# Row maxima split into high and low before the turn, one handover for unit 0, and four weight loads moved on SyncE

## The chip, the cores and the metric

The kernel runs on one core of one Trainium2 chip. The metric is device time in microseconds. The kernel before takes 1729.69 us (median of three runs, 1728.79 to 1730.18).

The five engines are named as the profile names them: PE is TensorE, with PEld its weight loads; DVE is VectorE, ACT ScalarE, POOL GpSimd and SP SyncE. SP computes nothing here; it issues the DMAs, one after the other, and waits in its queue for the data of each.

## The reference

One transformer block whose two layer norms are modulated by a condition vector `c`. All of it is float32.

```python
mod = (silu(c) @ w_mod).reshape(1, 6, 1, 512)
sa, ca, ga, sb, cb, gb = (mod[:, i] for i in range(6))
h = layernorm(x) * (1 + ca) + sa
x = x + ga * attention(h)          # 32 heads of 16, one shared key and value head
h = layernorm(x) * (1 + cb) + sb
x = x + gb * ((sigmoid(h @ w_gate) * (h @ w_up)) @ w_down)
```

with S = 2048 rows of D = 512, F = 1792, and attention as

```python
q = (h @ wq).reshape(1, S, 32, 16).transpose(0, 2, 1, 3)
k, v = h @ wk, h @ wv              # S x 16 each
scores = einsum("bhqd,bkd->bhqk", q, k) * 16 ** -0.5
o = einsum("bhqk,bkd->bhqd", softmax(scores, axis=-1), v)
return o.transpose(0, 2, 1, 3).reshape(1, S, 512) @ wo
```

The softmax subtracts the row's maximum over the 2048 keys, so each of the 32 x 2048 rows of scores needs its maximum before the exponentials are taken.

## The kernel before

**Units.** The attention is cut into 32 units: four query blocks of 512 rows (`b` = 0 to 3), and in each eight units of four heads. Every score is computed twice. A tile `sa` has 128 queries on the partitions and 512 keys in the row; VectorE reduces it to one maximum per query (`mx`). A unit has 64 such tiles. A tile `st` has 128 keys on the partitions and 512 queries in the row; ScalarE takes its exponential to `P`, and TensorE multiplies `P` with the values into `c`. `sa` tiles run A0 = 80 tiles ahead of the `st` tiles, that is one unit and a quarter.

**How a maximum gets into the exponential.** The query operand `qp` of a unit holds, beside the queries' high and low fp16 parts, two rows for the maxima: high part and low part, each in fp16 and divided by SM = 16. The product `st` thereby comes out with the maximum already subtracted. The way of a maximum from `mx` (query on the partition) to these rows (query along the row) is here called the handover. `max_end` has VectorE reduce four partial maxima of each of 16 columns to `m16`, 128x16; `max_rows` has TensorE turn it (fp32, by the identity matrix) into a score bank `pm`, copies it out, makes the two parts, and has SP write them to `qp` with four DMAs. In the steady part ScalarE copies it out and GpSimd makes the parts; in the opening VectorE makes them from the bank. In the steady part the handover of a unit is called one step after the last of its `sa` tiles: `max_end` before the step's scores, `max_rows` in its middle.

**Queries.** The query projection `q` (four 128-column groups per block, 12 matmuls each, three to a piece in the opening) is split into high and low, written to DRAM (`qD`), and read back in `qp`'s layout by six DMAs for each pair of units. All of this is issued by SP.

**Order.** Instructions on TensorE, VectorE and ScalarE keep the order in which the program writes them (`Ordered`, `keep`), as do those issued through `pool1` on GpSimd. Those issued through `pool` and `sp` are placed by the scheduler of the language. The opening, up to 108 us, is one written string of tokens, `PLAN`: `lm` loads 1 MB of `w_mod`, `lw` a part of `wq`, `lx` a block of `x`; `q` is a third of a query group, `QA` and `QL` its high and low part; `a` is an `sa` product and `x` its maximum; `pm`, `me`, `pr`, `m` use a loaded part of `w_mod`; `mx` is a handover of unit 0. In the opening there are four `sa` banks, afterwards three, and two for `st`.

**Steps.** After the opening each step takes 128 keys: four `st` and four `sa` tiles alternate, with the value product of an earlier step and one or more pieces of other work between them. In block 0 these are the query projections of the other blocks, while GpSimd splits the weights of the second half into fp16 high and low parts and SP writes them to DRAM (`wst`, `gw`, `wD`). From unit 8 on they are the output projection and the second half of the previous block.

Of the kernel before, what the change touches and what calls it, by code (L numbers as in the profile page):

```python
# [78 lines left out]
def adaln_mqa_glu_kernel(  # L79
# [105 lines left out]
    make_identity(nc, ident)  # L185
    mhalf = cp.tile([P, 1], F32, name="mhalf")
# [17 lines left out]
    def load_mod(i):  # L204
        t_ = pro.tile([P, NDC, D], F32, tag="wm", name="wm", bufs=4)
        sp.dma_start(t_, w_mod[:, i * D:(i + 1) * D].rearrange("(k p) n -> p k n", p=P))
        wmods[i] = t_
# [323 lines left out]
    def a_max(i, n, sa):  # L531
        kc, qt = n // 16, n // 4 % 4
        j, pr = heads[n % 4]
        dve.tensor_reduce(mxs[i][:, 2 * j + pr, qt, kc:kc + 1], sa, axis=AX.X, op=ALU.max)
        if i > 0 and n == 63:
            pend.append((i, 0, 4))
# [13 lines left out]
    def max_rows(i, t0, t1, m16):  # L550
        qp, pr0 = get_q(i)
        nt = t1 - t0
        n = 4 * nt
        pm = sbank("sa")
        pe.transpose(pm[:n, :P], m16, ident)
        mh = wp.tile([n, 2, P], F16, tag="mh", name="mh", bufs=4)
        if not first:
            m32 = wp.tile([n, P], F32, tag="m32", name="m32", bufs=4)
# [3 lines left out]
        else:  # L562
            dve.tensor_scalar(mh[:, 0], pm[:n, :P], 1.0 / SM, None, op0=ALU.mult)
            dve.scalar_tensor_tensor(mh[:, 1], pm[:n, :P], 1.0 / SM, mh[:, 0],
                                     op0=ALU.mult, op1=ALU.subtract)
        for j in range(2):
            for h in range(2):
                r = 64 * j + 48 + h
                sp.dma_start(qp[r:r + 1, pr0:pr0 + 2, t0 * P:t1 * P], mh[2 * nt * j:2 * nt * (j + 1), h, :])
# [279 lines left out]
    groups = {}  # L849
# [10 lines left out]
    def q_end(b, o):  # L860
# [9 lines left out]
              "a": a_next, "x": lambda: a_max(*held.pop(0)), "mx": lambda t: max_end(0, t, t + 1)(),  # L870
              "lw": load_wq, "lx": load_x, "lm": load_mod, "bl": lambda: blanks.append(blank(pool1))}
# [204 lines left out]
```

## Time and profile before

| | |
|---|---|
| median of three runs | 1729.69 us |
| profiled execution | 1730.8 us, its span 1729.0 us |
| mean granted clock | 0.991 |
| TensorE busy | 1689.2 us, 98% |
| TensorE weight loads | 574.4 us, 33% |
| VectorE busy | 1431.1 us, 83% |
| ScalarE busy | 1232.7 us, 71% |
| GpSimd busy | 610.7 us, 35% |

A trace is one profiled execution. In a list of instructions a row begins with the start in us and the length in us, then the engine, the line, the operation, `out<-in`, the shapes and the count. What stands in square brackets is how long the engine had been idle before it and who ended the wait. The line L128 stands for every instruction that went through `Ordered`. A row of SPq is a stretch of time that SP's queue spent issuing DMAs of one kind. A row of the chain of waits is a start, a length, an engine and a tile: the work that the end of the run depended on, in order of time.

### The profile page before, as it was taken

To read this page: it belongs to the slowest core of one execution; us is meant where nothing else is said; L and a number is where in the kernel's file an instruction comes from. 1 tells how busy PE (TensorE), PEld (TensorE's weight loads), DVE (VectorE), ACT (ScalarE), POOL (GpSimd) and SP (SyncE) were. 2 spreads that over 40 slices of the span, in tenths; PEclk is the share of its full clock that TensorE was granted. 3 is DMA by queue.
4 is the path that set the end of the run, shared out by engine and by line. 5 is a ranking of instruction groups with operands and counts; after the bars stand their busy time and mean duration, and the time that the engine had idled before them with its cause. 6 is when DMAs were issued, how large, how long until landed. Compare 5 with 4: busy or idle time off the path is not lost.

```text
span 1729.0 us, 34862 instructions
## 1 busy us (share of the span) xinstructions
PE 1689.2 (98%) x13971; PEld 574.4 (33%) x13971; DVE 1431.1 (83%) x2371; ACT 1232.7 (71%) x2253; POOL 610.7 (35%) x720
## 2 busy tenths in 40 slices
PE   6989999999999999999999999999999999999998
PEld 3423333233223333333333333333333333323443
DVE  8889999899998888888898998898898888931311
ACT  4448888788878777777778777777778777774100
POOL 4341463543454231332154232233254141231533
PEclk9899999999999999999999999999999999999999
DMA  8021332320101010111011110011101010111211
GB/s 284 1 89 35 107 97 79 114 93 23 57 24 44 30 51 11 38 45 36 26 41 32 41 48 15 26 48 49 33 23 51 30 56 5 30 50 56 76 59 49
DMA packets 66282, 90.88 MB, mean 53 GB/s; under 512 B 14800, under 2 KB 41424, under 8 KB 66120
## 3 DMA queue, kind: packets, MB, share of 16 engines
q1 hardware_dynamic: 66120, 88.66, 16.2%
q8 instruction: 109, 1.79, 0.4%
q14 instruction: 53, 0.43, 0.1%
HBM read 67.68 MB, written 16.22 MB: 49 GB/s over the span
## 4 chain that ended last, share of the span: by engine, by line
PE 87%; DVE 4%; DMA 3%; POOL 2%; ACT 2%; issue 1%; SPq 1%; POOLq 0%; ACTq 0%; DVEq 0%
PE c L128 27%; PE st L128 21%; PE pgu L128 12%; PE sa L128 9%; PE pd L128 5%; PE pgu L152 4%; DVE mx L128 3%; PE pq L128 2%; PE pd L152 2%; PE po L128 2%; ACT P L128 1%; DMA wst<-in_B_w_up_dram 1%; PE pt L128 1%; DMA xall<-in_A_x_dram 1%; PE po L152 1%
## 5 line engine op out<-in xcount | busy, mean ns | idle before, releaser
L128 DVE TENSOR_REDUCE mx<-sa 128x1 f32<-128x512 f32 x2048 | 1289.6, 685 | 121.2 <-PE sa L128 114.3
L128 ACT ACTIVATE P<-st 128x512 f32<-128x512 f32 x2048 | 1135.0, 596 | 285.7 <-PE sa L128 250.4
L128 PE MATMUL st<-qp,kp 64*128 64x512 f16 x2048 | 748.4, 380 | 9.5 <-DMA qp<-mh 5.3
L128 PE MATMUL sa<-kp,qp 64*128 64x512 f16 x2048 | 749.2, 384 | 7.4 <-DVE mx L128 4.0
L128 PE MATMUL c<-P,V 128*32 128x512 f32 (+1 forms) x5296 | 578.3, 509 | 0.9 <-ACT cs L128 0.2
L128 PEld LDWEIGHTS <-kp 64*128 64x128 f16 x2048 | 177.0, 94 | 510.4 <-issue 416.9
L128 PEld LDWEIGHTS <-qp 64*128 64x128 f16 x2048 | 186.5, 93 | 171.1 <-issue 79.9
L128 PE MATMUL pgu<-h2h,gw 64*128 64x512 f16 x1344 | 242.9, 376 | 0.0
L128 PEld LDWEIGHTS c<-P,V 128*32 128x32 f32 x5296 | 104.5, 108 | 189.1 <-issue 180.2
L796 POOL TENSOR_SCALAR th<-th 128x512 f32<-128x512 f32 x42 | 25.9, 617 | 353.7 <-ACT th L128 353.7
L128 PE MATMUL pgu<-h2l,gw 64*128 64x512 f16 x672 | 133.3, 376 | 0.0
L128 PEld LDWEIGHTS <-gw 64*128 64x128 f16 x2016 | 100.0, 94 | 81.6 <-issue 4.1
L152 PE MATMUL pgu<-h2h,gw 128*128 128x512 f16 x224 | 66.9, 379 | 1.2 <-POOL h2h L303 1.2
L497 POOL MEMSET qp<- 32x2048 f16 x28 | 50.3, 1798 | 49.5 <-issue 30.0
L802 POOL TENSOR_TENSOR gl<-th,gh 128x512 f16<-128x512 f32 x56 | 64.7, 1155 | 4.1
L790 ACT ACTIVATE th<-pgu 128x512 f32<-128x512 f32 x14 | 8.4, 597 | 79.3 <-PE pgu L152 79.3
L799 DVE SCALAR_TENSOR_TENSOR th<-th,pgu 128x512 f32<-128x512 f32 x14 | 9.6, 688 | 66.0 <-PE pgu L152 51.9
L272 POOL TENSOR_SCALAR wst<-wst 128x512 f32<-128x512 f32 x46 | 28.4, 618 | 98.9 <-DMA wst<-in_B_w_gate_dram 41.7
L128 DVE COPY u<-pgu 128x512 f32<-128x512 f32 x42 | 28.6, 681 | 38.6 <-PE st L128 22.6
L819 POOL TENSOR_TENSOR ot<-ot,gb 128x512 f32<-128x512 f32 x10 | 12.7, 1271 | 132.0 <-ACT ot L128 132.0
L659 POOL TENSOR_TENSOR raw<-raw,rb 128x512 f32<-128x512 f32 x15 | 19.1, 1272 | 105.4 <-DMA rb<-lD 67.4
L797 POOL TENSOR_TENSOR th<-th,u 128x512 f32<-128x512 f32 x42 | 53.3, 1270 | 3.5
(157 smaller groups left out, 1314.0 us busy)
## 6 DMA issues: line engine op xcount, KB each, us to landing
gw<-wD SPq DMA_DIRECT2D x56, 512.0 KB
wD<-gw SPq DMA_DIRECT2D x14, 512.0 KB
wm<-in_w_mod_dram SPq DMA_DIRECT2D x6, 1024.0 KB
qp<-qD SPq DMA_DIRECT2D x96, 64.0 KB
qD<-q SPq DMA_DIRECT2D x16, 256.0 KB
raw<-cs SPq DMA_DIRECT2D x128, 32.0 KB
xr<-in_A_x_dram SPq DMA_DIRECT2D x16, 256.0 KB
out_dram<-ot SPq DMA_DIRECT2D x16, 256.0 KB
```

The source lines that it names most:

```text
L128: return (lambda *a, **k: keep(f_(*a, **k))) if pinned else f_
L152: pe.matmul(self.bank, l_, r_, start=(n == 0), stop=(n == self.n - 1))
L272: pool.tensor_scalar(w_, w_, SW, 0.0, op0=ALU.mult, op1=ALU.add)
L497: eng.memset(qp[j:j + 32], 0.0)
L659: keep(pool.tensor_tensor(raw, raw, rb, op=ALU.mult))
L790: act.activation(th, p_, AF.Tanh, scale=0.5 / (SH * SW))
L796: pool.tensor_scalar(th, th, 1.0, 1.0, op0=ALU.add, op1=ALU.mult)
L797: pool.tensor_tensor(th, th, u_, op=ALU.mult)
L799: dve.scalar_tensor_tensor(th, th, 1.0, p_, op0=ALU.add, op1=ALU.mult)
L802: pool.tensor_tensor(lo, th, hi, op=ALU.subtract)
L819: pool.tensor_tensor(ot, ot, mods[5], op=ALU.mult)
```

## The change

Three things change together.

*The split.* `max_end` now lets VectorE make the two parts from the unturned `m16`, in a tile `mhl` of 128x2x16 fp16: one `tensor_scalar` for the high part, one `scalar_tensor_tensor` for the low part. `max_rows` turns both with one fp16 matmul against a new fp16 identity, `ident16`, into 32x128 of a score bank; ScalarE copies these to `mh` (fp16), and four DMAs write the rows as before. The two GpSimd instructions of a handover go, and so do VectorE's two in the opening. `ident16` is one more GpSimd instruction at the start.

*Unit 0.* Its four handovers of 128 queries each (`mx0` to `mx3`) become one for all 512, in two tokens: `mx` is VectorE's part, `my` TensorE's, ScalarE's and SP's. The last part of `PLAN` is written anew.

*The loads.* The four loads `lm4 lm3 lm2 lm5` move from the head of the plan to behind the first `a`, and are issued through `sp1`, which keeps the order of the program.

```diff
 PLAN = (
-    'lw0 lx2 lx3 lw1 lw2 lw3 lm4 lm3 lm2 lm5 pm1 S00 S01 me1 ...
+    'lw0 lx2 lx3 lw1 lw2 lw3 pm1 S00 S01 me1 ...
...
-    '... ra3 E12 a H13 rb3 pk10 x E13 pk11 '
+    '... ra3 E12 a lm4 lm3 lm2 lm5 H13 rb3 pk10 x E13 pk11 '
...
-    'x a q013 x a x a QA01 q020 mx0 a x q021 QL01 a x q022 x a q023 x a mx1 q030 QA02 x a q031 x a QL02 x a q032 x '
-    'a q033 mx2 x a q100 QA03 x a q101 x QL03 a x a q102 mx3 a x q103 x a QA10 q110 x a q111 x QL10 a x a q112 x a '
-    'q113 x a x a QA11 x a x a QL11 x a x a x a x x x '
+    'x a q013 x a x a QA01 q020 x a q021 x QL01 a x q022 x a a q023 x a q030 QA02 x a x a q031 x QL02 a q032 x a '
+    'q033 a x QA03 a q100 x a q101 mx QL03 x a my q102 x a x a q103 x a q110 QA10 x a q111 x a QL10 x a q112 x a '
+    'q113 x a x a QA11 x a x a QL11 x a x x x '
 )
...
+    ident16 = cp.tile([P, P], F16, name="ident16")
+    pool.tensor_scalar(ident16, ident, 1.0, 0.0, op0=ALU.mult, op1=ALU.add)
...
-            pend.append((i, 0, 4))
+            pend.append((i,))
...
-    def max_end(i, t0, t1):
-        nt = t1 - t0
-        n = 4 * nt
-        m16 = wp.tile([P, n], F32, tag="m16", name="m16", bufs=4)
-        dve.tensor_reduce(m16.rearrange("p (h t) -> p h t", t=nt), mxs[i][:, :, t0:t1, :], axis=AX.X, op=ALU.max)
-        return lambda: max_rows(i, t0, t1, m16)
+    def max_end(i):
+        m16 = wp.tile([P, 16], F32, tag="m16", name="m16", bufs=4)
+        mhl = wp.tile([P, 2, 16], F16, tag="mhl", name="mhl", bufs=4)
+        dve.tensor_reduce(m16.rearrange("p (h t) -> p h t", t=4), mxs[i], axis=AX.X, op=ALU.max)
+        dve.tensor_scalar(mhl[:, 0], m16, 1.0 / SM, None, op0=ALU.mult)
+        dve.scalar_tensor_tensor(mhl[:, 1], m16, 1.0 / SM, mhl[:, 0], op0=ALU.mult, op1=ALU.subtract)
+        return lambda: max_rows(i, mhl)
...
-        pe.transpose(pm[:n, :P], m16, ident)
...
-            act.activation(m32, pm[:n, :P], AF.Identity, scale=1.0 / SM)
-            pool.tensor_scalar(mh[:, 0], m32, 1.0, 0.0, op0=ALU.mult, op1=ALU.add)
-            pool.tensor_tensor(mh[:, 1], m32, mh[:, 0], op=ALU.subtract)
...
+        pe.matmul(pm[:32, :P], mhl.rearrange("p h m -> p (h m)"), ident16, start=True, stop=True)
+        mh = wp.tile([32, P], F16, tag="mh", name="mh", bufs=4)
+        act.activation(mh, pm[:32, :P], AF.Identity)
         for j in range(2):
             for h in range(2):
                 r = 64 * j + 48 + h
-                sp.dma_start(qp[r:r + 1, pr0:pr0 + 2, t0 * P:t1 * P], mh[2 * nt * j:2 * nt * (j + 1), h, :])
+                sp.dma_start(qp[r:r + 1, pr0:pr0 + 2, :], mh[16 * h + 8 * j:16 * h + 8 * j + 8, :])
```

The order of instructions shows three places. A row is the line, the operation, `out<-in`, the shape and, behind an x, how many stand in a row.

The first is SP's queue in the opening; `wm` is a loaded part of `w_mod`, `q_...` a split query group, `qp<-mh` the rows of maxima. Before:

```order
L206 DMA wm<-in_w_mod_dram 128x4x512 x4
L479 DMA qD<-q_308 128x2x512
L505 DMA qp<-qD 16x4x512 x6
L569 DMA qp<-mh 1x2x128 x4
L479 DMA qD<-q_990 128x2x512
L569 DMA qp<-mh 1x2x128 x4
L479 DMA qD<-q_1047 128x2x512
L505 DMA qp<-qD 16x4x512 x2
L569 DMA qp<-mh 1x2x128 x4
L479 DMA qD<-q_1092 128x2x512
L505 DMA qp<-qD 16x4x512 x2
L569 DMA qp<-mh 1x2x128 x4
```

And in the changed kernel:

```order
L483 DMA qD<-q_302 128x2x512
L509 DMA qp<-qD 16x4x512 x6
L128 DMA wm<-in_w_mod_dram 128x4x512 x4
L483 DMA qD<-q_992 128x2x512
L509 DMA qp<-qD 16x4x512 x5
L483 DMA qD<-q_1030 128x2x512
L509 DMA qp<-qD 16x4x512
L483 DMA qD<-q_1062 128x2x512
L564 DMA qp<-mh 1x8x128 x4
```

The four loads now stand behind the first query write and its six reads, and the one row of unit 0 behind the third of the later query writes.

The second is VectorE from the last value copy (`V`) to the handover of unit 1; `m_...` are the reduced maxima (`m16`). Before, where the group of reduction, two parts from the bank and four maxima comes four times:

```order
L128 TENSOR_REDUCE mx<-sa 128x1 x6
L128 TENSOR_REDUCE m_998<-mx 128x4
L128 TENSOR_SCALAR mh<-sa 4x128
L128 SCALAR_TENSOR_TENSOR mh<-sa,mh 4x128
L128 TENSOR_REDUCE mx<-sa 128x1 x4
L128 TENSOR_REDUCE m_1032<-mx 128x4
```

And in the changed kernel, where it comes once:

```order
L128 TENSOR_SCALAR V<-pv 128x4x16
L128 TENSOR_REDUCE mx<-sa 128x1 x18
L128 TENSOR_REDUCE m_1078<-mx 128x16
L128 TENSOR_SCALAR mhl<-m_1078 128x16
L128 SCALAR_TENSOR_TENSOR mhl<-m_1078,mhl 128x16
L128 TENSOR_REDUCE mx<-sa 128x1 x64
L128 TENSOR_REDUCE m_1614<-mx 128x16
L128 TENSOR_SCALAR mhl<-m_1614 128x16
L128 SCALAR_TENSOR_TENSOR mhl<-m_1614,mhl 128x16
```

The parts are no longer read from a score bank, so nothing of TensorE stands between the row reduction and them; in the steady part VectorE's queue has two instructions more per unit.

The third is SP's queue around the start of unit 5, where rows, a query write and a weight write meet. Before:

```order
L479 DMA qD<-q_4213 128x2x512
L569 DMA qp<-mh 1x8x128 x2
L688 DMA wD<-gw 128x2048
L569 DMA qp<-mh 1x8x128 x2
L631 DMA lD<-cs 4x512
```

And in the changed kernel:

```order
L483 DMA qD<-q_4184 128x2x512
L564 DMA qp<-mh 1x8x128 x4
L683 DMA wD<-gw 128x2048
L626 DMA lD<-cs 4x512
```

All four rows now stand ahead of the weight write, but behind the same query write. Elsewhere the order on TensorE, VectorE, ScalarE and GpSimd is the one before, but for the instructions named.

More of the change, by code (lines that the diff above doesn't have):

```diff
@@ L202, in load_x, with load_mod @@
         sp.dma_start(xall[:, 4 * b:4 * b + 4, :], x[b * QB:(b + 1) * QB, :].rearrange("(t p) d -> p t d", p=P))
-    def load_mod(i):
+    sp1 = Ordered(nc.sync)
+    def load_mod(i, eng=sp):
         t_ = pro.tile([P, NDC, D], F32, tag="wm", name="wm", bufs=4)
-        sp.dma_start(t_, w_mod[:, i * D:(i + 1) * D].rearrange("(k p) n -> p k n", p=P))
+        eng.dma_start(t_, w_mod[:, i * D:(i + 1) * D].rearrange("(k p) n -> p k n", p=P))
         wmods[i] = t_
@@ L847, in a_next @@
         apos += 1
-    groups = {}
+    groups, rows = {}, []
     def q_part(b, o, k):
@@ L869, in adaln_mqa_glu_kernel @@
               "pm": mod_product, "me": mod_copy, "pr": mod_sum, "m": mod_end,
-              "a": a_next, "x": lambda: a_max(*held.pop(0)), "mx": lambda t: max_end(0, t, t + 1)(),
-              "lw": load_wq, "lx": load_x, "lm": load_mod, "bl": lambda: blanks.append(blank(pool1))}
+              "a": a_next, "x": lambda: a_max(*held.pop(0)), "mx": lambda: rows.append(max_end(0)), "my": lambda: rows.pop()(),
+              "lw": load_wq, "lx": load_x, "lm": lambda i: load_mod(i, sp1), "bl": lambda: blanks.append(blank(pool1))}
     for tok in PLAN.split():
```

11 lines of the change are left out of this document (1 added, 10 removed), and 10 rows, old and new, of the table PLAN.

## The prediction

> **What bounds the kernel now.** I read the busy time by stretch first, then the chain of waits of the opening, then the places where a row of maxima is handed over.
>
> ```profile
> 105.00:450.00 345.00, 333.87 (x3375) 106.23 (x3374) 332.13 (x545) 295.77 (x553) 151.17 (x186) 0.98 0.25 81
> 450.00:1560.00 1110.00, 1108.11 (x9239) 362.28 (x9237) 973.95 (x1583) 867.24 (x1585) 363.39 (x424) 1.00 0.12 35
> ```
>
> The columns are the window, its length, and the busy time of TensorE, weight loads, VectorE, ScalarE and GpSimd, then granted clock and DMA. In the first query block (units 0 to 7) TensorE and VectorE are both at 96 to 97%; from 450 us on TensorE has 1108.1 of 1110 us and VectorE 88%. So TensorE's order of work sets the time, VectorE stands close behind it, and the edit puts two more instructions on VectorE. The chain of waits shows the end of the opening, where the last query products run.
>
> ```profile
> 81.84 0.75 PE pq L128 x3
> 82.91 0.75 PE pq L128 x3
> ...
> 105.08 0.75 PE pq L128 x3
> 106.20 4.88 DVE mx L128 x8
> ```
>
> The 20 product pieces (three matmuls each) start 1.07 us apart when nothing stops them. From the first to the twentieth they need 105.08 - 81.84 = 23.24 us where 19 x 1.07 = 20.33 would do: 2.9 us are waits. Then eight maxima in 4.88 us, 0.61 each, are the end of the opening.
>
> **1. Four small handovers become one (opening).** Each old handover looks like this on VectorE:
>
> ```profile
> 85.37 0.17 DVE L128 TENSOR_REDUCE m<-mx 128x4 f32<-128x16 f32 x1
> 87.04 0.28 DVE L128 TENSOR_SCALAR mh<-sa 4x128 f16<-4x128 f32 x1 [1.49 <-PE sa L128]
> 87.56 0.67 DVE L128 TENSOR_REDUCE mx<-sa 128x1 f32<-128x512 f32 x1
> ```
>
> VectorE waits in its own queue for TensorE's transposition (1.49 us here), no maximum is taken meanwhile, and TensorE then lacks a score bank. The new one splits on VectorE before the product, ScalarE evicts it, and VectorE waits for nobody. TensorE at 1.07 us a piece is then the bound: the 2.9 us go, less 0.1 us for the one product that stays. Behind the last piece stood seven score tiles (73 of 80 done at q113 in the plan), now five (75 of 80): two maxima at 0.61 fewer, 1.2 us. Sum -4.0 us. Bounds: nothing, if something else is late there, and -5.5, if all of the four holes of about 2 us less one of 0.6 and the tail came back. The row's four DMAs now stand behind the third query write on SP; what hides them is worked out under the rivals.
>
> One GpSimd copy of 128x128 (`ident16`) comes in ahead of the opening's zeroing. It costs about 0.3 us there, an estimate: a quarter of the 1.15 us that a 128x512 pass takes below. TensorE's first product waits for its load:
>
> ```profile
> 8.02 1.94 PE L128 MATMUL pmod<-wm,cbc 128*32 128x512 f32 x8 [8.02 <-DMA wm<-in_w_mod_dram]
> ```
>
> So 0, and 0.3 if VectorE's silu, which waits for that zeroing, were later than the load.
>
> **2. Late modulation loads behind the queries' trip.** Four loads of 1 MB each were ahead of the query write.
>
> ```profile
> 18.56 5.54 SPq L206 DMA_DIRECT2D wm<-in_w_mod_dram  x4
> 30.54 0.37 SPq L479 DMA_DIRECT2D qD<-q  x1
> 37.09 2.67 SPq L505 DMA_DIRECT2D qp<-qD  x6
> ```
>
> ```profile
> 40.40 0.58 PE L128 MATMUL sa<-kp,qp 64*128 64x512 f16 x1 [1.27 <-DMA qp<-qD]
> ```
>
> The write needs 37.09 - 30.54 = 6.55 us and could lose about 4 of them, but TensorE waited only 1.27 us for the queries; its work ahead of them is late for another reason. And VectorE, full from 41 to 60 us, gains less still:
>
> ```profile
> 41.63 0.23 DVE L128 TENSOR_TENSOR nw<-rs 128x4 f32<-128x4 f32 x1
> 41.90 1.07 DVE L128 SCALAR_TENSOR_TENSOR nw<-nw,ve 128x4 f32<-128x4 f32 x1
> ```
>
> ```profile
> 39.71 1.01 POOL L128 TENSOR_TENSOR rs<-ve,mhalf 128x4 f32<-128x4 f32 x1 [2.30 <-DVE ve L128]
> 40.69 3.38 POOL L128 TENSOR_TENSOR h1l<-h,h1h 128x512 f16<-128x512 f32 x3
> ```
>
> The first maximum at 41.02 would start near 39.7, but the instruction after it needs `rs`, done at 40.72, when GpSimd has already begun its three two-input instructions, and the small VectorE ones end with each of these (41.86, 42.97). They end there in both kernels. I take -0.15 us; the ends are 0 and -1.3. The loads are now issued behind the six query reads, near 36 us. Before, they were all in within 18.5 us of their first issue (18.56, and the write behind them landed by 37.09), so they are in by 55; the plan reads the first of them behind the fourth block's key products and two value products, so nobody waits: no cost, and up to 2 us if that cover were gone.
>
> **3. Two more VectorE instructions in each of 31 handovers.** No 128x16 split exists in the trace. The nearest rows are 128x4:
>
> ```profile
> 13.49 0.16 DVE L128 SCALAR_TENSOR_TENSOR nw<-nw,ve 128x4 f32<-128x4 f32 x1
> 13.69 0.16 DVE L128 SCALAR_TENSOR_TENSOR rs<-nw,rs 128x4 f32<-128x4 f32 x1
> ```
>
> Dependent ones start 0.20 apart. Now the next maximum follows the row reduction by 0.14 us (140.80 to 140.94, below); behind reduction, split and difference it starts at 0.25 + 0.20 + 0.10 = 0.55, so VectorE is 0.41 us later (bounds 0.35 and 0.6). What TensorE loses shows in unit 1:
>
> ```profile
> 140.80 0.22 DVE L128 TENSOR_REDUCE m<-mx 128x16 f32<-128x64 f32 x1
> 141.54 0.68 DVE L128 TENSOR_REDUCE mx<-sa 128x1 f32<-128x512 f32 x1
> ```
>
> ```profile
> 141.61 0.28 PE L128 MATMUL sa<-ident,m 128*16 128x128 f32 x1
> 141.82 0.39 PE L128 MATMUL st<-qp,kp 64*128 64x512 f16 x1
> 142.27 0.37 PE L128 MATMUL sa<-kp,qp 64*128 64x512 f16 x1
> ```
>
> The handover takes one of three score banks, so the second score product after it (142.27) waits for the maximum that ends at 141.54 + 0.68 = 142.22: 0.05 us later it starts. A VectorE that is 0.41 late makes TensorE 0.41 late, and the transposition, which held TensorE from 141.61 to 141.82, gives nothing back here though a half-precision product may hold it 0.15 us less. The eight handovers of the first block are all alike: 3.3 us. From unit 9 on there are two kinds:
>
> ```profile
> 949.61 0.68 DVE L128 TENSOR_REDUCE mx<-sa 128x1 f32<-128x512 f32 x1
> 1141.86 1.28 DVE L128 TENSOR_REDUCE mx<-sa 128x1 f32<-128x512 f32 x2
> ```
>
> ```profile
> 950.92 0.38 PE L128 MATMUL sa<-kp,qp 64*128 64x512 f16 x1
> 1142.60 0.37 PE L128 MATMUL sa<-kp,qp 64*128 64x512 f16 x1
> ```
>
> At 950.92 the bank has been free since 950.29: 0.63 us of slack, the delay is hidden and 0.15 gained. At 1142.60 it has been free since about 1142.54: 0.41 lost. Read so at each of the 23, eight are of the second kind (8 x 0.41 = 3.3), the other fifteen have 0.3 to 0.7 us of slack and come to about -0.6 together. Sum 2.7 us; bounds -3.5 (all gain 0.15) and +9.4.
>
> **4. GpSimd leaves the chain of the row.** TensorE waits for rows three times, 5.26 us in all:
>
> ```profile
> 192.54 0.37 PE L128 MATMUL st<-qp,kp 64*128 64x512 f16 x1 [0.73 <-DMA qp<-mh]
> ...
> 317.04 0.58 PE L128 MATMUL st<-qp,kp 64*128 64x512 f16 x1 [3.74 <-DMA qp<-mh]
> ...
> 401.70 0.37 PE L128 MATMUL st<-qp,kp 64*128 64x512 f16 x1 [0.79 <-DMA qp<-mh]
> ```
>
> ```profile
> 185.85 2.57 SPq L688 DMA_DIRECT2D wD<-gw  x2
> 311.71 0.36 SPq L479 DMA_DIRECT2D qD<-q  x1
> 314.51 1.31 SPq L569 DMA_DIRECT2D qp<-mh  x2
> 397.72 2.77 SPq L569 DMA_DIRECT2D qp<-mh  x4
> ```
>
> Two GpSimd instructions per row go, but the row's DMAs keep their place in SP's queue. In unit 2 they stand behind two weight writes, which end at 188.42 as before: the 0.73 us stay. In unit 5 they stand behind a query write that is issued at 311.71; four issues of 0.65 from 312.1 end at 314.7 instead of 315.82: 1.1 of 3.74 us go. In unit 7 no DMA that waits stands ahead of the row at 397.72, which waited for GpSimd alone: all of 0.79 goes. So -1.9 us, not -5.3. The stalls that stay also swallow the 0.41 us of units 2 and 5, so 3.3 becomes 2.5.
>
> **5. VectorE and GpSimd get in each other's way.** The pair at 41.9 above shows it: a 0.16 us instruction with two inputs in SBUF took 1.07 beside a GpSimd TENSOR_TENSOR. The new split and difference are of that sort. What GpSimd does at that moment, unit by unit, gives two hits that are not swallowed:
>
> ```profile
> 902.39 0.22 DVE L128 TENSOR_REDUCE m<-mx 128x16 f32<-128x64 f32 x1
> ```
>
> ```profile
> 222.91 1.15 POOL L274 TENSOR_TENSOR gw<-wst,gw 128x512 f16<-128x512 f32 x1
> 902.16 2.10 POOL L298 TENSOR_SCALAR t<-xr,mv,rs 128x512 f32<-128x512 f32 x1
> ```
>
> In unit 3 the difference would run near 223.0 (its row reduction is at 222.5) and end with this at 224.06: 1.1 us. In unit 18 the split would begin at 902.64, and GpSimd is busy until 904.26: 1.6 us, if a TENSOR_SCALAR holds VectorE as a TENSOR_TENSOR does. No row shows that, so the ends are 0 and 1.6; the held pair at 41.9 is the nearest row, and I take 1.6. With 0.3 us for a shorter one in unit 7 that makes 3.0; bounds 0 and 8.
>
> The Trainium skill ("SBUF — State Buffer", section "Who interferes with whom") says that GpSimd and VectorE share one pair of ports as an exclusive lock, held for the whole instruction by whichever starts first, and that a VectorE instruction with two SBUF inputs meets it against any GpSimd instruction that reads SBUF. By it the sum keeps its 1.6; by a reading in which only TENSOR_TENSOR holds VectorE it would be 1.6 less, 1730.3. The rule speaks against the change, since the new pair goes just where it applies.
>
> **Sum:** -4.0 - 0.15 + 2.5 + 2.7 - 1.9 + 3.0 = +2.15 us. The profiled execution (1730.8 us, span 1729.0) would become 1733.0; against the median of the three runs, 1729.69, 1.1 lower, I forecast 1731.9. The runs lie within 0.08%, so 0.2% (3.5 us) is about what a measurement can tell from no change; the forecast, +0.13%, is inside.
>
> **Rivals.** *Hidden handover* (faster): TensorE gets the lost 0.41 us back because its own queue is loose elsewhere. For it: VectorE idles 136 us between 450 and 1560. Against: a TensorE that is busy 1108 of 1110 us has nothing to catch up with. Terms 3 and 5 vanish: 1729.7 - 4.15 - 1.9 = 1723.6. It decides when less than 0.1 us per handover reaches TensorE.
>
> *Port at every turn* (slower): the phases of GpSimd shift and the first block, where GpSimd is busy 151 of 345 us, hits in most units. Six more at 1.1 give 1738.5. It decides from two more hits on. Against: from unit 9 on GpSimd is mostly idle at that moment.
>
> *The trip was the bound*: the 4 us of the shorter write reach the end, 1728.0. Against: 1.27 us of waiting and rows 41.63 and 41.90.
>
> *The opening gives nothing*: the one row for unit 0 lands later than the first did, and the first scores wait for it; 1735.9. Against: the product stands behind the 14th piece, 81.84 + 14 x 1.07 = 96.8; with 0.7 us for the eviction and the query write, four issues of 0.65 and the 1.2 us from the last issue to the score in unit 5 (315.82 to 317.04), the row is in at 101.3, and the scores of unit 0 began at 108.44, now 104.4.
>
> **Chances.** The forecast 0.42 (its own range 1728 to 1735, by the bounds of the VectorE delay and of one hit more or less), hidden handover 0.22, port at every turn 0.20, trip 0.08, opening 0.08. Of the forecast's 0.42 about 0.10 lies above 1733.2 and 0.03 below 1726.2. Faster: 0.22 + 0.03 = 0.25; slower: 0.20 + 0.08 + 0.10 = 0.38; the rest, 0.37, within. The range 1724 to 1737 leaves out half of the hidden handover and part of the port case.
>
> **What would show it.** After: mhl rows near 0.17 us, 31 of them without a GpSimd neighbour; query products 1.07 us apart throughout; first scores of unit 0 near 104.4 instead of 108.44; the first score product near 39.2 and the maximum train after 44 us unmoved; rows of unit 5 still waited for. Wrong if the split instructions take 0.5 us or more in many units, if units of the first block grow by more than 0.5 us, or if the wait for rows is gone entirely.

## The result: slightly faster, where slightly slower was forecast

| | kernel before | changed kernel |
|---|---|---|
| median | 1730.01 us (22 runs, 1728.20 to 1733.74) | 1728.21 us (22 runs, 1724.16 to 1732.46) |
| profiled execution | 1730.8 us, span 1729.0 us | 1730.2 us, span 1728.4 us |

The ratio is 0.9989, with a 95% interval of 0.9982 to 0.9997: 1.9 us faster, between 0.5 and 3.1. The forecast was 1731.9 us, 0.13% slower. Single executions scatter over 5.5 us (before) and 8.3 us (changed); what part of this is the clock is told at the end. The two profiled executions differ by 0.6 us only, because the one of the changed kernel lies 2.0 us above its median and the one before 0.8 above its own. What follows is the account of these two executions.

Where the time went is read best at the first score product (`st`) of each unit, which both kernels have at the same place in TensorE's order:

| first `st` of unit | before | after | difference | of which in this stretch |
|---|---|---|---|---|
| 0 (end of the opening) | 108.44 | 104.62 | -3.82 | -3.82 |
| 3 | 232.24 | 231.86 | -0.37 | +3.45 |
| 7 | 400.31 | 397.60 | -2.70 | -2.33 |
| 8 | 441.96 | 438.72 | -3.24 | -0.54 |
| 31 | 1535.63 | 1535.00 | -0.63 | +2.61 |
| end of the span | 1728.99 | 1728.38 | -0.61 | +0.02 |

So the opening gained 3.8 us. The first block took 0.6 us longer, which is the net of large steps of both signs, and the long steady part took 2.6 us longer. The busy times of the changed kernel in the two stretches that the prediction began with:

```profile
105.00:450.00 345.00, 336.73 (x3397) 106.73 (x3395) 335.84 (x561) 298.25 (x556) 147.49 (x174) 0.99 0.25 80
450.00:1560.00 1110.00, 1107.22 (x9209) 364.22 (x9208) 977.55 (x1624) 865.05 (x1580) 346.15 (x375) 1.00 0.11 35
```

The columns are those of the prediction's table. VectorE has 3.7 us more work in the first stretch and 3.6 in the second, GpSimd 3.7 and 17.2 less. A handover in the changed kernel looks like this (unit 1, list of instructions in order of time):

```profile
137.14 0.22 DVE L128 TENSOR_REDUCE m<-mx 128x16 f32<-128x64 f32 x1
137.40 0.17 DVE L128 TENSOR_SCALAR mhl<-m 128x16 f16<-128x16 f32 x1
137.60 0.18 DVE L128 SCALAR_TENSOR_TENSOR mhl<-m,mhl 128x16 f16<-128x16 f32 x1
137.70 1.88 DVE L128 TENSOR_REDUCE mx<-sa 128x1 f32<-128x512 f32 x3
137.84 0.23 PE L128 MATMUL sa<-ident,mhl 128*32 128x128 f16 x1
138.00 0.39 PE L128 MATMUL st<-qp,kp 64*128 64x512 f16 x1
138.10 0.27 ACT L128 ACTIVATE mh<-sa 32x128 f16<-32x128 f32 x1
138.39 0.65 SPq L564 DMA_DIRECT2D qp<-mh  x1
```

Reduction to next maximum takes 0.56 us where it took 0.14: VectorE is 0.42 us later. The product holds TensorE 0.16 us (137.84 to 138.00), the fp32 transposition held it 0.21. The first row DMA is issued 1.25 us after the reduction began.

### The profile page after: what moved, and what is told of

It is laid out like the page before. It is cut to its first block, busy times and chain, and to the rows that moved or that the text cites. A ratio compares the mean times of both kernels' runs of the same rounds, so it can differ in the third digit from the quotient of the medians.

```text
span 1728.4 us, 34828 instructions
## 1 busy us (share of the span) xinstructions
PE 1690.8 (98%) x13968; PEld 576.7 (33%) x13968; DVE 1441.5 (83%) x2424; ACT 1234.2 (71%) x2254; POOL 590.7 (34%) x659
## 4 chain that ended last, share of the span: by engine, by line
PE 81%; DVE 14%; ACT 2%; issue 1%; DMA 1%; POOL 0%; SPq 0%; POOLq 0%; DVEq 0%; ACTq 0%
PE c L128 25%; PE st L128 19%; PE pgu L128 12%; DVE mx L128 11%; PE sa L128 8%; PE pd L128 5%; PE pgu L152 4%; PE pd L152 2%; ACT P L128 2%; PE po L128 2%; PE pq L128 2%; PE pt L128 1%; DVE st L128 1%; DMA xall<-in_A_x_dram 1%; PE po L152 1%
## 5 line engine op out<-in xcount | busy, mean ns | idle before, releaser
L128 PE MATMUL pgu<-h2h,gw 64*128 64x512 f16 x1344 | 247.1, 376 | 0.3 <-DVE ot L128 0.2
```

The source lines that it names most:

```text
L128: return (lambda *a, **k: keep(f_(*a, **k))) if pinned else f_
```

## The experiments

Each is a change to the kernel named; ratios are to the kernel before, with 95% intervals. "Us faster" or "slower" is worked out from these ratios. The kernel before was run anew beside each group of runs: its median was 1729.7 us beside the first four, 1730.5 beside the next four and 1733.1 beside the last three, where its 17 executions fell into two groups, 1728.4 to 1729.9 and 1733.1 to 1734.0. Ratios of different groups can therefore differ by up to 0.2% for this reason alone. Two questions lead: which of the three parts moved the time, and why the handovers cost less than forecast.

**The new handover alone.** The opening and the loads of before; from unit 1 on the new `max_end` and `max_rows` (here `max_rows2`), and `ident16` for them.

```diff
         dve.tensor_reduce(m16..., mxs[i][:, :, t0:t1, :], ...)
-        return lambda: max_rows(i, t0, t1, m16)
+        if first:
+            return lambda: max_rows(i, t0, t1, m16)
+        dve.tensor_scalar(mhl[:, 0], m16, 1.0 / SM, None, op0=ALU.mult)
+        dve.scalar_tensor_tensor(mhl[:, 1], m16, 1.0 / SM, mhl[:, 0], ...)
+        return lambda: max_rows2(i, mhl)
```

> Plan and loads of the kernel before, with only the new handover in units 1 to 31 (split on VectorE, one half-precision product). Theory A (the opening gained about 3.8 us and the handovers gave about 3.2 of it back; each handover costs what of its 0.41 us on VectorE is not covered by the slack of the second score product behind it): 1.5 to 3.5 us slower than before, the first scores of unit 0 unmoved at 108.4, the growth per unit from unit 9 on as between the two profiles (+0.36 to +0.43 in units 14, 15, 22, 23, 24, 27, 28, about -0.1 in the others), the rows of unit 5 waited for 1.6 instead of 3.7 us, one idle stretch of TensorE of about 1 us in unit 3. Theory B (the handover is the gain, the opening gives nothing): 1 to 2 us faster than before, no growth of 0.4 in those units.

Measured: 1732.41 us, ratio 1.0019 (1.0008 to 1.0030), 3.3 us slower. The handover by itself is a loss, so theory B falls. The growth of every unit from 9 on repeats the one between the two profiles within 0.02 us (table below). The first scores of unit 0 came at 110.46 and not at 108.4: in this execution TensorE ran 10.2 us at half clock between 51 and 62 us, where before had 6.8 between 66 and 77. In unit 5 the scores waited 0.36 us for rows, less than the expected 1.6; unit 3 had its idle stretch, 0.97 us.

**The new opening alone.** The changed kernel with GpSimd's handover in units 1 to 31.

```diff
         dve.tensor_reduce(m16..., mxs[i], ...)
+        if not first:
+            return lambda: max_rows_g(i, m16)
```

`max_rows_g` is the `max_rows` of before: fp32 turn, ScalarE's copy, two parts by GpSimd.

> The changed kernel's opening and loads, with the handover of before in units 1 to 31 (ScalarE copies out, GpSimd makes the parts). Theory A: 2 to 4 us faster than the changed kernel, that is 3.5 to 5 us faster than before, with the first scores of unit 0 at 104.6 and every unit from 9 on as long as before; in unit 5 the rows are waited for 3 to 4 us again and TensorE's clock is halved for some us behind that. Theory B: about the time of before or slower.

Measured: 1727.21 us, ratio 0.9977 (0.9966 to 0.9989), 4.0 us faster than before. From unit 9 to 31 it takes as long as before within 0.23 us. The wait for rows in unit 5 is back, 3.77 us, with TensorE at half clock from 310 to 317 us. The opening is the gain, and the 4.0 us (interval 1.9 to 5.9) fit the forecast of 4.15.

The first scores of unit 0 came at 101.98 and not at 104.6 as expected. The profiles tell the two apart. From the first late query product to the first scores of unit 0 the two profiles with the old opening take 26.67 us, and all eleven with the new one 22.56 to 22.60: the new end of the opening gains 4.1 us every time. What comes ahead of that first product varies: it starts at 81.8 and 83.8 us with the old opening, and anywhere from 77.0 to 82.4 with the new one, with different stretches of half clock ahead of it.

**The loads back at the head.**

```diff
-    'lw0 lx2 lx3 lw1 lw2 lw3 pm1 ...
+    'lw0 lx2 lx3 lw1 lw2 lw3 lm4 lm3 lm2 lm5 pm1 ...
-    ... E12 a lm4 lm3 lm2 lm5 H13 ...
+    ... E12 a H13 ...
...
-              "lm": lambda i: load_mod(i, sp1), ...
+              "lm": load_mod, ...
```

> The changed kernel with the four loads back at the head of the plan. If the loads give nothing at the end of the opening (theory A: their 1.5 us at the first score product are lost again by the query products): within 0.8 us of the changed kernel; first score product back near 40.4, first scores of unit 0 at 104.3 to 104.9. If the loads carry the gain of the opening (rival C): 1.5 us or more slower than the changed kernel, first scores of unit 0 at 106 or later.

Measured: 1728.24 us, ratio 0.9986 (0.9974 to 0.9999), the same as the changed kernel. The first score product is back at 40.17 us. The first scores of unit 0 came at 101.65, which is earlier than expected for either theory, but the end of the opening is again 22.60 us long: it is the start of the query products that came earlier. By the ratio the two kernels are the same, so rival C falls, and the loads gave nothing that these runs can tell apart from their scatter (1723.8 to 1732.6 us).

**The split made twice.** A second pair of the same two VectorE instructions per handover, into a tile that nothing reads: a direct price for VectorE's lateness.

```diff
         dve.scalar_tensor_tensor(mhl[:, 1], m16, 1.0 / SM, mhl[:, 0], ...)
+        if not first:
+            dve.tensor_scalar(mh2[:, 0], m16, 1.0 / SM, None, op0=ALU.mult)
+            dve.scalar_tensor_tensor(mh2[:, 1], m16, 1.0 / SM, mh2[:, 0], ...)
```

> The changed kernel with the split of units 1 to 31 made a second time on VectorE into a tile that nothing reads: VectorE is 0.82 instead of 0.41 us later at each handover. Theory A, with the slack of the second score product behind each handover as read in the kernel before (0.05 us in units 1 to 8, 14, 15, 22 to 24, 27, 28; 0.28 to 0.74 in the others): units 9 to 30 grow by 10.4 us against before where they grew by 2.6, units 1 to 8 by 3 more; 9 to 11 us slower than the changed kernel. Rival (TensorE catches up behind a late VectorE): under 2 us slower.

Measured: 1739.95 us, ratio 1.0060 (1.0046 to 1.0074), 11.7 us above the changed kernel's median. TensorE does not catch up. In the profile units 9 to 30 grew by 8.2 us against before instead of 10.4, and units 1 to 8 by 6.5, which is 6.0 more than in the changed kernel where 3 were expected; three pieces of half clock lie among them where the changed kernel has one. Where the slack said 0.77 us (units 22 to 24) only 0.33 came; why is open.

How much longer than in the kernel before it takes from the first `st` of one unit to the first `st` of the next, from the profiles. A row is named by the unit that starts at the end of the stretch; that unit's handover lies in it.

| unit that starts | changed | handover alone | opening alone | split twice | late low part | early low part |
|---|---|---|---|---|---|---|
| 9 | -0.11 | -0.10 | 0.00 | +0.18 | +0.06 | +0.06 |
| 14 | +0.36 | +0.37 | +0.02 | +0.65 | +1.04 | +0.02 |
| 15 | +0.36 | +0.36 | +0.01 | +0.92 | +1.05 | +0.01 |
| 18 | +0.55 | +0.56 | 0.00 | +0.84 | +0.09 | +0.09 |
| 20 | -0.02 | -0.01 | +0.02 | +0.27 | 0.00 | 0.00 |
| 23 | +0.43 | +0.43 | +0.01 | +0.33 | +1.00 | +0.04 |
| 27 | +0.38 | +0.38 | +0.02 | +0.65 | +1.06 | +0.03 |
| 9 to 31 together | +2.61 | +2.77 | +0.23 | +8.04 | +6.58 | +0.51 |

The last two columns are runs that follow.

**The low part two maxima later.** The idea: keep VectorE's work away from the two maxima for which TensorE waits. ScalarE makes the high part. The cuts of this run and of the early low part show the calls where they run; the functions that carry them there are left out.

```diff
             scores(0)
+            act.activation(mhl[:, 0], m16, AF.Identity, scale=1.0 / SM)
...
             scores(1)
+            dve.scalar_tensor_tensor(mhl[:, 1], m16, 1.0 / SM, mhl[:, 0], ...)
...
-            max_rows(i, mhl)
             scores(2)
...
             scores(3)
+            max_rows(i, mhl)
```

> The changed kernel, but in units 1 to 31 ScalarE makes the high part (behind the first exponential of the step), VectorE only the low part, two maxima later, and the product that turns them stands behind the step's fourth score product. Theory A (a handover costs what VectorE is late at the second score product behind the row reduction): nothing stands any more between the reduction and the two maxima that TensorE waits for, so units 14, 15, 22, 23, 24, 27 and 28 lose their 0.36 to 0.43 us, all others keep their gain of up to 0.15, and the half-clock stretch behind unit 3 cannot come from the split: 4 to 8 us faster than the changed kernel, 1720 to 1724. Rival D (VectorE's total work counts, it has no slack in the first eight units): half of the 0.41 us stays there, 2 to 4 us faster. Rival E (nothing but the clock's chance moves the time): the same as the changed kernel.

Measured: 1729.63 us, ratio 0.9997 (0.9986 to 1.0008): not the 4 to 8 us below the changed kernel that were expected, and no different from before within the interval. Units 14, 15, 16, 23, 24 and 27 now lose about 1 us each. The list of instructions around the handover of unit 14 shows why:

```profile
703.57 0.68 DVE L128 TENSOR_REDUCE mx<-sa 128x1 f32<-128x512 f32 x1
704.16 1.23 DVE L128 SCALAR_TENSOR_TENSOR mhl<-m,mhl 128x16 f16<-128x16 f32 x1
...
704.09 1.27 POOL L796 TENSOR_TENSOR th<-th,u 128x512 f32<-128x512 f32 x1
```

The low part begins 0.07 us after GpSimd's TENSOR_TENSOR and ends with it, at 705.39 against 705.36. The same GpSimd instruction, which needs VectorE's copy of `u`, lies beside the low part in each of these units (1.10 to 1.23 us there), so the hit repeats.

**Two row DMAs for four.** As above; the columns of `mhl` are ordered so that both rows of one half go out in one DMA.

```diff
-            for h in range(2):
-                r = 64 * j + 48 + h
-                sp.dma_start(qp[r:r + 1, pr0:pr0 + 2, :], mh[16 * h + 8 * j:16 * h + 8 * j + 8, :])
+            r = 64 * j + 48
+            sp.dma_start(qp[r:r + 2, pr0:pr0 + 2, :], mh[16 * j:16 * j + 16, :])
```

> The same, and the four row DMAs of a handover become two of two rows each: SP issues for about 1.3 instead of 2.6 us. If the issues set the wait for rows in unit 5, that wait is 1.3 us shorter than in the kernel with four; the rest of the program within 0.1 us per unit. In the order a weight write now stands ahead of the rows of unit 5; if that write's data are the later ones, the wait grows instead. Overall within 1.5 us of the kernel with four.

Measured: 1728.55 us, ratio 0.9986 (0.9973 to 1.0000). From unit 9 to 27 every unit is as long as with four DMAs, within 0.02 us (in unit 28 the low part met GpSimd once more, 1.0 us). In unit 5 the wait did not shrink (3.79 us in one piece, against 3.17 + 0.53). The rows stood behind the query write and a weight write, and here the query write was issued 1.8 us later than with four DMAs (305.56 against 303.73), so this run alone does not say what the issues cost; the run with the rows ahead of the query write does.

**TensorE kept busy at the end of the opening.** To the changed kernel ten products are added whose results nothing reads, in TensorE's waits between 101 and 107 us.

```diff
-    '... QL11 x a x x x '
+    '... QL11 x w w a x x x '
...
+    WARM = (0, 4, 0, 2, 1, 0, 1, 0)
...
                 st_tile(i, kb, n // 2, n % 2)
+                if s < 2:
+                    warm(WARM[4 * s + n])
```

A `w`, and each of `warm`'s, is one product of `kp` with `kp`: in the plan into a spare bank, in the steps into the bank of `c` before its first use.

> The changed kernel with ten products more on TensorE whose results nothing reads, placed in the waits at the end of the opening (two ahead of the last score product of the plan, eight in the first two steps). If TensorE's clock is halved because it had idled (0.56 + 0.99 + 0.58 us within 3 us): the two half-clock stretches of 3.4 us each behind 105 us go, VectorE no longer idles 1.4 us around 110 us, and the kernel is 1 to 2 us faster than the changed one, everything behind unit 1 unmoved. Rival F (the clock falls there whatever TensorE does, or the products are in the way): no gain, or up to 2 us slower.

Measured: 1724.68 us, ratio 0.9961 (0.9946 to 0.9975). The table by window for the changed kernel, and then for this one (columns: window, length, busy time of TensorE, weight loads, VectorE, ScalarE, GpSimd, granted clock, DMA share, GB/s):

```profile
104.60:107.00 2.40, 1.34 (x8) 0.42 (x8) 2.40 (x5) 1.15 (x3) 1.90 (x3) 1.00 1.00 345
107.00:113.90 6.90, 6.39 (x31) 1.56 (x34) 6.19 (x11) 4.98 (x9) 6.34 (x9) 0.51 0.34 106
```

```profile
101.80:104.20 2.40, 1.94 (x14) 0.89 (x13) 2.40 (x5) 1.11 (x3) 1.83 (x3) 1.00 0.96 343
104.20:111.10 6.90, 6.70 (x45) 2.05 (x43) 6.90 (x12) 6.00 (x11) 6.34 (x9) 1.00 0.35 106
```

The 6.9 us at half clock are gone and VectorE no longer idles; unit 1 starts 1.25 us earlier after unit 0 than in the changed kernel. In all ten profiles without the products TensorE falls to half clock here, for 3.4 or 6.8 us; in all three with them it does not. So rival F falls: what TensorE does in its waits decides the clock here. The ratios of the two kernels differ by more, 0.0028 or 4.8 us, though their intervals come within 1.2 us of each other. The two profiles differ by 5.3 us: 2.8 of them stand already at the first scores of unit 0 (101.86 against 104.62), and 1.2 come from unit 3, where the half clock of the changed kernel is missing. Both of these differ between executions of other kernels too, so only the 1.25 us are shown to be the products' doing.

**The three together, with the late low part.**

> Late low part, two row DMAs and the ten products together: if the three act in different places they add up, 1 to 2 us faster than without the products, 1719 to 1722.

Measured: 1727.76 us, ratio 0.9984 (0.9974 to 0.9994), well above the expected 1719 to 1722. The products help here too (unit 1 starts 1.6 us earlier after unit 0 than without them), but units 9 to 31 keep the 7.6 us of the late low part with two DMAs.

**Rows ahead of the query write.** In the changed kernel the query writes of the first block are issued two steps later (`first` is the opening, where they stay), and the rows keep the program's order on SP (`sp1`).

```diff
-        sp.dma_start(qD[...], q2)
+        def write():
+            (sp if first else sp1).dma_start(qD[...], q2)
+
+        if first:
+            write()
+        else:
+            defer(2, write)
...
-                sp.dma_start(qp[r:r + 1, pr0:pr0 + 2, :], mh[...])
+                sp1.dma_start(qp[r:r + 1, pr0:pr0 + 2, :], mh[...])
```

> The changed kernel, with the query writes of units 0 to 7 issued two steps later, so that in SP's queue the rows of unit 5 stand ahead of both query writes instead of behind them; nothing else moves. If the query write held those rows: TensorE's wait for rows at the start of unit 5 (0.99 + 0.65 us in the changed kernel) is gone, and with it any half-clock stretch there; 0.5 to 2.5 us faster than the changed kernel. If the four row DMAs themselves are the long part: the wait stays.

Measured: 1726.80 us, ratio 0.9971 (0.9958 to 0.9983). SP's queue and TensorE at the start of unit 5:

```profile
297.49 2.71 SPq L128 DMA_DIRECT2D qp<-mh  x4
300.29 3.12 SPq L128 DMA_DIRECT2D qD<-q  x2
...
306.32 0.39 PE L128 MATMUL st<-qp,kp 64*128 64x512 f16 x1
```

The rows are issued 8.8 us ahead of the score that needs them, and it waits for nothing, although there are four issues as before. So the query write ahead of them was the wait. By the medians this kernel is 1.4 us below the changed one, by the ratios 3.1.

**The low part one maximum earlier.** Same as the late one, but directly behind the first maximum of the step.

```diff
             scores(0)
             act.activation(mhl[:, 0], m16, AF.Identity, scale=1.0 / SM)
+            dve.scalar_tensor_tensor(mhl[:, 1], m16, 1.0 / SM, mhl[:, 0], ...)
...
             scores(1)
-            dve.scalar_tensor_tensor(mhl[:, 1], m16, 1.0 / SM, mhl[:, 0], ...)
```

> The changed kernel, but in units 1 to 31 ScalarE makes the high part, VectorE the low part directly behind the first maximum of the step (one maximum earlier than in the run that put it behind the second), and the product stands behind the step's fourth score product. In the run with the later place the low part took 1.1 to 1.2 us in units 14, 15, 16, 23, 24 and 27, where GpSimd had just begun a TENSOR_TENSOR. Port theory: at the earlier place no GpSimd TENSOR_TENSOR runs in those units, the low part takes 0.17 us there, and each of them starts 0.9 to 1.1 us earlier; units 9 to 31 then take as long as in the kernel before within 0.5 us together, 2 to 3 us less than in the changed kernel; a hit stays likely in units 3 and 5. 2 to 6 us faster than the changed kernel. If the length has another cause (the strided fp16 input, ScalarE's half of the work): still about 1.1 us in those units and no gain.

Measured: 1725.70 us, ratio 0.9959 (0.9942 to 0.9975). In unit 14 again:

```profile
706.93 0.17 DVE L128 SCALAR_TENSOR_TENSOR mhl<-m,mhl 128x16 f16<-128x16 f32 x1
...
708.05 1.27 POOL L797 TENSOR_TENSOR th<-th,u 128x512 f32<-128x512 f32 x1
```

The low part is done 0.95 us before that TENSOR_TENSOR begins. Units 14, 15, 16, 23, 24 and 27 start 1.03, 1.03, 0.81, 0.96, 0.95 and 1.03 us earlier than with the late place, and units 9 to 31 take 0.5 us more than before instead of 2.6. The same instruction, one maximum apart in VectorE's order, takes 1.23 us or 0.17. The expected gain of 2 to 6 us over the changed kernel came: 2.5 by the medians, 5.2 by the ratios.

**The version that beats both.** Early low part, rows ahead of the query writes in two DMAs, and the ten products.

> The early low part, rows ahead of the query writes with two DMAs per handover, and the ten products that keep TensorE busy at the end of the opening. If the places are independent, the sum of the three: 1718 to 1722.

Measured: 1718.95 us (1717.4 to 1719.5), ratio 0.9923 (0.9910 to 0.9937): 13 us faster than the kernel before beside it, 11 us below the median of the first comparison, and inside the expected 1718 to 1722. In its profile TensorE never falls to half clock between the end of the opening and the last microseconds.

## Why the prediction was wrong, step by step

The forecast had the sign wrong. The step that failed is term 4, the rows: it was put at -1.9 us and measured -6.0 in the profiles. Its largest missing piece is a cost that no term of the sum and no rival had, the half clock of TensorE behind a wait. The opening came out as forecast (4.0), but what was forecast as +6.3 us for the handovers (terms 3 to 5) is +3.3 by itself (handover alone) and +2 on top of the opening (changed kernel against opening alone).

**The bound.** Right: TensorE's order sets the time, and VectorE's lateness of 0.42 us reaches it as 0.36 to 0.43 where no slack stands. (A second split in the same place gave less regular steps, 0.33 to 0.92.) The hidden-handover rival fell with the split made twice.

**Term 1, the opening, -4.0.** Right, in its parts too: -3.82 at the first score of unit 0 (104.62, forecast near 104.4) and 4.0 in the run of the opening alone. The chain of waits of the changed kernel:

```profile
82.09 0.75 PE pq L128 x3
...
102.66 0.75 PE pq L128 x3
...
103.79 3.68 DVE mx L128 x6
```

From the first to the twentieth product piece it takes 20.57 us, where 20.33 was the bound and 23.24 the time before; at the end stand six maxima (3.68 us) instead of eight (4.88). That the first scores came so near to the forecast 104.4 is luck: the other ten profiles with this opening have them between 99.58 and 104.98.

**Term 2, the loads, -0.15.** As small as forecast, as far as the runs can tell. The trip shrank as worked out, 4.2 us:

```profile
30.46 0.37 SPq L483 DMA_DIRECT2D qD<-q  x1
32.78 2.67 SPq L509 DMA_DIRECT2D qp<-qD  x6
...
51.04 0.37 PE L128 MATMUL sa<-kp,qp 64*128 64x512 f16 x1 [2.93 <-DVE mx L128]
```

The first score product started at 38.87 (forecast near 39.2), but TensorE then ran into VectorE: 2.93 us of waiting at 51.04, where it was 0.66 before:

```profile
50.64 0.37 PE L128 MATMUL sa<-kp,qp 64*128 64x512 f16 x1 [0.66 <-DVE mx L128]
```

By the first late query product the changed kernel was 0.26 us behind. The run with the loads back at the head has the same time within its interval of about 2 us to each side; a finer value no run here shows.

**Term 3, 0.41 us per handover.** Right for units 9 to 31. VectorE is 0.42 us later. Eight units were to lose 0.41: seven lose 0.36 to 0.43 (14, 15, 22, 23, 24, 27 and 28), and unit 18 0.55, with its small hit. Of the other fifteen, unit 16 loses 0.19 and the rest lie between -0.17 and +0.10; seven of them gain 0.10 to 0.17, near the 0.15 that the prediction put in without a row for it. The sum is +2.6, forecast 2.7. In the first block it was too small: the stalls that were to swallow the 0.41 us of units 2 and 5 went away or shrank, so the eight handovers, with up to 0.2 us that follows behind some, cost 4.1 us where 2.5 was forecast.

**Term 4, rows, -1.9. This step failed.** At the first few scores of units 2, 5 and 7 the changed kernel gained 0.77, 4.25 and 0.95 us, 6.0 in all. Unit 7 was nearly right (0.79). In unit 2 I had the weight writes end at the same time as before; the second is issued at 184.78 instead of 188.09, 3.3 us earlier, and the rows with it, while the unit starts only 2.7 us earlier; the 0.73 us go. (Why GpSimd had their data ready sooner is open.) SP's queue there in the changed kernel:

```profile
182.55 2.56 SPq L683 DMA_DIRECT2D wD<-gw  x2
185.21 2.76 SPq L564 DMA_DIRECT2D qp<-mh  x4
```

In unit 5 the four issues do follow the query write as forecast, at 312.29:

```profile
311.88 0.36 SPq L483 DMA_DIRECT2D qD<-q  x1
312.29 2.71 SPq L564 DMA_DIRECT2D qp<-mh  x4
...
314.83 0.37 PE L128 MATMUL st<-qp,kp 64*128 64x512 f16 x1 [0.99 <-DMA qp<-mh]
...
316.09 0.39 PE L128 MATMUL st<-qp,kp 64*128 64x512 f16 x1 [0.65 <-DMA qp<-mh]
```

But the first score needs only the rows of its half, the first two issues, and starts before the fourth has ended (312.29 + 2.71 = 315.00); the two waits together are 1.64 us, not 2.6: 2.1 us of waiting went, not 1.1. The other half of the 4.25 us was left out of the sum altogether: what the long wait did to TensorE afterwards. By window, before and after:

```profile
317.00:322.40 5.40, 5.36 (x32) 1.15 (x32) 2.97 (x5) 2.62 (x5) 0.00 (x0) 0.50 0.00 0
```

```profile
316.00:322.00 6.00, 5.81 (x62) 1.89 (x62) 5.25 (x9) 4.91 (x10) 0.00 (x0) 1.00 0.22 86
```

Before, the 3.74 us of idling were followed by 5.4 us at half clock, 32 products where the changed kernel did 62 in 6.0. A wait of TensorE was priced at its length; it cost 4.25 - 2.10 = 2.15 us more. So the 4.1 us that term 4 lacked are 2.15 for the clock, 1.0 for the wait in unit 5, 0.8 for unit 2 and 0.2 for unit 7. The wait in unit 5 was there in five other profiles, 2.6 to 3.8 us long, and the half clock followed it in each.

**Term 5, VectorE and GpSimd, +3.0.** Its sum is near to what this profile shows, by luck: one large part did not come, and half clock that the term did not have made up for it. Unit 3 was forecast at 1.1 and cost 2.5 beyond the handover itself:

```profile
219.31 0.98 DVE L128 TENSOR_SCALAR mhl<-m 128x16 f16<-128x16 f32 x1
220.33 0.54 DVE L128 SCALAR_TENSOR_TENSOR mhl<-m,mhl 128x16 f16<-128x16 f32 x1
...
219.11 1.16 POOL L278 TENSOR_TENSOR gw<-wst,gw 128x512 f16<-128x512 f32 x1
220.24 0.62 POOL L277 TENSOR_SCALAR gw<-wst 128x512 f16<-128x512 f32 x1
...
220.93 0.23 PE L128 MATMUL sa<-ident,mhl 128*32 128x128 f16 x1 [0.99 <-DVE mhl L128]
```

Both instructions end with GpSimd's; the forecast had only the second one held, by the next TENSOR_TENSOR. TensorE idles 0.99 us. Then the clock again:

```profile
221.00:223.00 2.00, 1.94 (x13) 0.37 (x14) 2.00 (x4) 1.46 (x3) 2.00 (x2) 1.00 0.08 35
223.00:226.40 3.40, 3.40 (x26) 0.70 (x26) 2.04 (x4) 1.62 (x3) 0.09 (x1) 0.52 0.34 136
```

3.4 us at half clock, about 1.5 us lost. That part is chance. Four other profiles have the same handover in this place: with the handover alone the half clock came too and unit 3 cost 2.5 us, while with the loads at the head, the ten products or the rows first TensorE idled 0.92 to 1.07 us, the clock stayed full, and unit 3 cost 0.9 to 1.1 us, about the 1.1 that was forecast. The hit of 1.6 us in unit 18 did not come:

```profile
899.94 0.30 DVE L128 TENSOR_SCALAR mhl<-m 128x16 f16<-128x16 f32 x1
900.27 0.17 DVE L128 SCALAR_TENSOR_TENSOR mhl<-m,mhl 128x16 f16<-128x16 f32 x1
...
899.45 2.10 POOL L302 TENSOR_SCALAR t<-xr,mv,rs 128x512 f32<-128x512 f32 x1
```

Both ran inside GpSimd's 2.10 us, and only the first lost 0.13. I took the upper end from a pair beside a TENSOR_TENSOR; the lower end, 0, was nearly right. The 0.3 us in unit 7 came on VectorE: the high part took 0.44 us there, 0.27 more than alone. The prediction's rule from the Trainium skill ("SBUF — State Buffer", section "Who interferes with whom"), that a VectorE instruction with two SBUF inputs meets any GpSimd instruction that reads SBUF, does not agree with the second of these rows (0.17 us inside the 2.10 us), and agrees with the second of unit 3. The first instruction of the pair has one tile as its input; the sentence cited does not cover it, and in unit 3 it was held all the same, 0.98 us.

**The sum.** By the two profiles: -3.82 for the opening, -6.0 for the rows with their clock, about +2.5 for unit 3, +2.6 for units 9 to 31, and the rest, +4.1, for the eight handovers of the first block (0.42 each and 0.1 to 0.2 behind some); together -0.6. Against the forecast: term 4 is 4.1 us too small and the hit in unit 18 1.5 too large; unit 3 (1.4) and the first block's handovers (4.1 for 2.5) cost more than forecast and take part of it back. Without the chance half clock in unit 3 this profile would lie some 1.5 us lower, nearer to the kernel's median.

## What to carry to other kernels

Price a wait of a TensorE that is otherwise full at its length and at what the granted clock shows for the 10 us from its start (here up to 6.8 us of half clock, beginning 1.7 to 3.5 us after the wait began); a few products that nothing reads, put into a wait that can't be removed, can be worth more than they cost. Where two engines get in each other's way, the place in the order decides: the same small VectorE instruction took 0.17 or 1.23 us for a shift of one maximum, so look at what GpSimd does at the new place in every unit before moving work there. Before removing an engine from a chain, look at whether the DMA queue behind it is held by something else; here one query write was the whole remaining wait.

## What the runs showed of the hardware

- *Half clock comes in pieces of 3.4 us.* In these traces the granted clock is 1.0 or 0.5, the latter for stretches of 3.4, 6.8 or 10.2 us. In units 1 to 8, over all profiles, TensorE had eight idle stretches of 0.97 to 1.27 us: behind four the clock fell (0.97, 0.99, 1.13 and 1.27 us), behind four it stayed full (0.99, 1.02, 1.04 and 1.07 us). In the run with the split made twice it fell behind a stretch of 0.78 us too, which came 0.5 us after one of 0.23. Behind six waits of 2.6 to 3.8 us it always fell, for 3.4 to 6.8 us. In the three runs with the late low part 17 waits of 0.96 to 1.04 us in units 14 to 28 left it full; what differs there is open. So in the first block a wait of 1 us costs about 1.5 us more, as in unit 3, or nothing, and which of the two is not explained here. The Trainium skill ("TensorE: Matmul & The Clock Gate", section "HAM oscillation — how this bites in real kernels") gives the rule "no PE-idle gaps >~3.4µs"; here 1 us was enough in four of eight cases.
- *Much of the scatter of single executions goes with the clock.* Of 29 executions of the kernel before, the eight with a mean granted clock of 0.990 took 1732.9 to 1734.2 us and the fifteen with 0.992 or more 1727.9 to 1729.7. In the changed kernel the link is looser: of its 22 executions the nine with 0.994 or more took 1724.2 to 1730.5 us, the four with 0.990 or 0.991 from 1727.6 to 1732.1, so something else moves the time there as well. Two executions with the same opening reached unit 0 at 108.44 and 110.46 us, with two and three pieces of 3.4 us between 46 and 105 us; from unit 9 on, kernels with the same handover agree within 0.02 us in nearly every unit. The best version's six runs lie within 2.1 us of each other, the others' within 4.5 to 11.9.
- *GpSimd holds VectorE for some instructions and not for others.* Beside a TENSOR_TENSOR of 1.16 to 1.27 us and a TENSOR_SCALAR of 0.62 us, the small VectorE instructions of the handover that began inside it did not end before it: 72 of 72 in the eleven profiles that have the new handover in units 1 to 31. Beside a TENSOR_SCALAR of 2.10 us that takes its scalars from tiles (`mv`, `rs`) none of 17 was held: the SCALAR_TENSOR_TENSOR took 0.17 or 0.18 us, the TENSOR_SCALAR 0.30 or 0.31. Why the two kinds of TENSOR_SCALAR differ is open.
